# Both heads of a pair in the two halves of the rows: 64x64 tiles of TensorE in a chunked attention, without block-diagonal copies

## The chip, the cores and the metric

One core of a Trainium2 chip runs the whole program. The metric is device microseconds of one execution; the time before is 1209.59 us, the median of 3 runs (1208.75 to 1212.22). Engines: PE is TensorE, DVE VectorE, ACT ScalarE, POOL GpSimd; SP only issues DMAs here.

## The reference

A recurrent attention feeds a mixture of experts, and that feeds a two-layer network. With 4 batches, 8 heads, 768 steps and head size 40:

```
for t in range(S):
    y[:, :, t] = einsum('bhd,bhde->bhe', r_t, state)
    Sa = einsum('bhde,bhe->bhd', state, a_t)
    state = state*w_t[:, :, None, :] - outer(Sa, b_t) + outer(v_t, k_t)
```

`y` as 3072 tokens of 320 is routed to one of 8 experts (320 to 1024 to 320, ReLU, scaled by the gate's probability), and the result goes through 320 to 2048 to 320 with a leaky ReLU. All is float32.

## The kernel before

**The attention** (class `Attn`, lines 536 to 890) cuts the 768 steps into 12 chunks of 64. The 32 heads are 16 pairs; `E`=40 is the head size, and a pair lies in `PW`=104 columns, head 0 in 0 to 39 and head 1 in 64 to 103. Chunks are worked two at a time (`kk`, 6 rounds in `run`, line 860). In a round:

- `a_load` and `kb_load` (643 to 661) load a, k and b with time on the rows and multiply them by running products of w (`pro`, `prod`). `K` has k in rows 0 to 63 and b in rows 64 to 127.
- `s1a` (662), for each of four groups of 4 pairs, transposes a on PE and copies the result out twice: into `abd`, a block-diagonal form in which each head's 64 columns have zeros at the other head's rows (two copies of 40x512), and into rows 64 to 103 of `XL` (four copies of 40x256).
- `s1` (678), for a chunk and a group, transposes K, copies it to `kbT`, and multiplies it by `abd` with all 128 rows: rows 0 to 63 of the result are masked into `XL` on DVE, rows 64 to 127 are copied and sent through memory (`LTd`) to the solver.
- `solver2` (704) turns all 32 heads of both chunks by substitution: 62 DVE instructions one after the other. `g_out` and `g_load` (709, 743) take the result through memory into `Gr`, for each pair a block-diagonal 128x128 matrix, and `wg` (767) fills its off-diagonal 32x32 blocks with matmuls on 32x32 tiles.
- `chain` (792), for a chunk and a group z of 4 pairs, carries the state. It has six steps on PE with evictions between them: transposes of v and r; transposes of the state `D0`; v and state times r (`VD`, `rb`, 4 matmuls, 104 columns of weights, 128 moving); `XL` times `R1` (8 matmuls of 128 rows and 64 columns); `Gr` times `X` (4 matmuls, 128x128); `K` times `R1` (8 matmuls of 128 rows and 64 or 40 columns). `R1` holds one head per column block, v's part in rows 0 to 63 and the state's part below, so the state and v are copied into it, and r is copied into `rb` in block-diagonal form. DVE masks, adds the state and writes `Y`; the decay goes to POOL or DVE.

A float32 matmul is two MATMUL passes in the trace, each with its own weight load.

**The experts** (class `Moe`, from 893) load weights in pieces into two buffers `raw`, split them in two parts (copies and subtractions on ACT, DVE, POOL) into three slots `w0`, `w1`, `w2`, and run PE. The same columns hold the attention's buffers before: `raw` and `abd` share columns of the region `pe`, and the slots hold `K`, `XL`, `Gr` and the solver's tiles.

**The order** is a list planner's (`Sched`, from line 100): every operation has a cost (`cost`, 183), a priority from a backward pass, and is put where it can start first. `copy` may go to ACT or DVE, `copy3` to ACT, DVE or POOL, `pv` to POOL or DVE; `tensor_tensor` on `nc.vector` stays on DVE. The matmuls of one step are one block and go out together. PSUM is 8 banks of 512 columns. Everything is emitted from lines 527 (blocks) and 529 (all else), so the trace's lines tell only these two apart and shapes tell the rest.

## Time and profile before

| what | value |
|---|---|
| median of 3 runs | 1209.59 us |
| the profiled execution | 1210.86 us, of which its span is 1209.0 us |
| busy, share of the span | PE 83%, PE's weight loads 74%, DVE 68%, ACT 53%, POOL 31% |
| instructions | 23474, of which MATMUL passes 8757 |
| mean granted clock of PE | 0.932 |
| DMA | 113.71 MB in 255413 packets |

How to read it: busy times are unions on one engine. The attention fills the first 560 us or so, the experts and the network the rest. A group of instructions is a line of code, an engine, an operation, names (w, f, plain are the slots and the plain region; bank is PSUM) and a shape; behind the bar stand its busy time in us, the mean of one in ns and the idle time before.

### The profile page before, as it was taken

Reading aid. Unit: us, or ns where it says so; the run is one execution under the profiler, and the core shown is the slowest. Engines: PE = TensorE matmul, PEld = TensorE weight load, DVE = VectorE, ACT = ScalarE, POOL = GpSimd, SP = SyncE. Lnnn points to the kernel's source line nnn. Section 1 sums busy time; section 2 is a strip of 40 time slices with the busy share of each in tenths; the row PEclk is TensorE's granted clock in tenths of the full one; section 3 lists DMA queues with packets and bytes.
Section 4 is the critical chain, followed back from the end, with each engine's and each line's share of the span. In section 5 each row is a group of like instructions: output and inputs, shape, how many; then the busy total and the mean of one; then the engine's idle time right before and its main releaser. Section 6 shows DMA issues by size and latency. Waiting matters only on the chain.

```text
span 1209.0 us, 23474 instructions
## 1 busy us (share of the span) xinstructions
PE 1009.3 (83%) x8757; PEld 897.0 (74%) x8757; DVE 826.9 (68%) x1681; ACT 641.9 (53%) x1473; POOL 376.8 (31%) x587
## 2 busy tenths in 40 slices
PE   2553787787877879789799999877999999999994
PEld 1352676676766767777699998867899999999994
DVE  5788687976879867757655559979655555555561
ACT  7885987797885968665544444434121212121230
POOL 9684266463553121222111112334001010110231
PEclk9875998989898989899799999987999999999998
DMA  9454365747638464933844444342100000000000
GB/s 163 110 152 112 77 103 109 141 93 145 107 80 174 76 141 114 253 89 113 217 130 133 126 113 120 109 147 82 66 1 23 11 22 18 17 6 17 12 7 31
DMA packets 255413, 113.71 MB, mean 94 GB/s; under 512 B 206784, under 2 KB 242416, under 8 KB 255097
## 3 DMA queue, kind: packets, MB, share of 16 engines
q1 hardware_dynamic: 251449, 100.25, 36.4%
q0 software_dynamic: 3840, 11.85, 2.9%
q8 instruction: 71, 1.16, 0.4%
q14 instruction: 53, 0.43, 0.1%
HBM read 81.08 MB, written 35.98 MB: 97 GB/s over the span
## 4 chain that ended last, share of the span: by engine, by line
PE 51%; ACT 15%; DVE 14%; DMA 8%; issue 5%; POOL 4%; SPq 2%; POOLq 0%; DVEq 0%; ACTq 0%
PE bank L529 41%; PE bank L527 11%; ACT w L529 8%; DVE plain L529 7%; DVE w L529 5%; ACT plain L529 5%; ACT f L529 2%; SPq L529 2%; DMA plain<-in_moe_w_in_dram 2%; DVE f L529 2%; POOL w L529 2%; DMA out_dram<-plain 1%; POOL f L529 1%; POOL plain L529 1%; DMA plain<-xs 1%
## 5 line engine op out<-in xcount | busy, mean ns | idle before, releaser
L529 PE MATMUL bank<-f,w 128*128 128x512 f32 (+2 forms) x1472 | 330.9, 365 | 6.7 <-ACT f L529 3.5
L529 PE MATMUL bank<-w,f 128*128 128x320 f32 (+1 forms) x1824 | 313.8, 314 | 10.7 <-ACT f L529 9.1
L529 PEld LDWEIGHTS bank<-w,f 128*128 128x128 f32 (+1 forms) x1824 | 284.7, 189 | 24.0 <-ACT f L529 10.8
L529 PEld LDWEIGHTS bank<-f,w 128*128 128x128 f32 x1472 | 254.3, 192 | 38.5 <-ACT f L529 4.3
L527 PE MATMUL bank<-plain,w 128*64 128x104 f32 (+3 forms) x1664 | 164.1, 280 | 51.6 <-ACT w L529 21.5
L527 PEld LDWEIGHTS bank<-plain,w 128*128 128x128 f32 (+2 forms) x1664 | 143.7, 170 | 70.9 <-ACT w L529 27.7
L529 ACT CAST f<-plain 128x512 fp32r<-128x512 f32 (+1 forms) x96 | 56.2, 586 | 240.1 <-PE bank L529 215.7
L529 DVE TENSOR_TENSOR w<-w 128x135 f32<-128x135 f32 (+20 forms) x401 | 154.3, 388 | 16.7 <-DMA w<-LTd 6.5
L529 DVE TENSOR_SCALAR plain<-bank,plain 128x512 f32<-128x512 f32 (+2 forms) x114 | 76.5, 672 | 123.4 <-PE bank L529 121.9
L529 ACT COPY w<-bank 40x256 f32<-40x256 f32 (+5 forms) x323 | 138.4, 436 | 23.2 <-PE bank L527 17.8
L529 DVE TENSOR_TENSOR plain<-bank,w 64x256 f32<-64x256 f32 (+2 forms) x192 | 87.6, 462 | 58.4 <-ACT f L529 19.0
L529 ACT COPY plain<-bank 104x256 f32<-104x256 f32 (+6 forms) x222 | 92.1, 432 | 25.9 <-PE bank L527 13.2
L529 POOL TENSOR_TENSOR w<-w 128x120 f32<-128x120 f32 (+4 forms) x133 | 93.5, 719 | 31.1 <-ACT w L529 19.0
L527 PE MATMUL bank<-ident,w 128*104 128x128 f32 x384 | 61.4, 297 | 39.5 <-POOL w L529 26.8
L529 ACT CAST w<-plain 128x640 fp32r<-128x640 f32 (+4 forms) x105 | 60.4, 591 | 63.4 <-DVE plain L529 29.6
L529 POOL DMA_INDIRECT ys<-plain x32 | 43.6, 1361 | 150.3 <-ACT plain L529 80.1
L527 PEld LDWEIGHTS bank<-ident,w 128*104 128x104 f32 x384 | 46.7, 141 | 46.2 <-POOL w L529 31.7
L529 DVE TENSOR_TENSOR w<-plain,w 128x512 fp32r<-128x512 f32 (+3 forms) x97 | 63.2, 655 | 24.4 <-ACT w L529 21.1
L529 POOL DMA_INDIRECT out_dram<-plain x24 | 25.9, 1079 | 151.3 <-ACT plain L529 110.7
L529 DVE SCALAR_TENSOR_TENSOR plain<-bank,plain 128x512 f32<-128x512 f32 (+1 forms) x112 | 68.5, 613 | 4.4
L529 ACT ACTIVATE f<-bank 128x480 fp32r<-128x480 f32 (+1 forms) x72 | 37.8, 530 | 63.3 <-PE bank L529 62.5
L529 DVE SCALAR_TENSOR_TENSOR f<-bank,f 128x480 fp32r<-128x480 f32 (+1 forms) x72 | 42.9, 601 | 36.3 <-ACT f L529 36.2
(110 smaller groups left out, 1334.9 us busy)
## 6 DMA issues: line engine op xcount, KB each, us to landing
plain<-in_moe_w_dram SPq DMA_DIRECT2D x32, 320.0 KB, 3.5
plain<-in_moe_w_dram SPq DMA_DIRECT2D x64, 128.0 KB, 2.7
LTd<-w SPq DMA_DIRECT2D x40, 128.0 KB, 2.3
plain<-in_moe_w_out_dram SPq DMA_DIRECT2D x8, 640.0 KB
xs<-w SPq DMA_DIRECT2D x8, 608.8 KB
plain<-xs SPq DMA_DIRECT2D x7, 603.8 KB, 5.4
plain<-in_moe_w_in_dram SPq DMA_DIRECT2D x8, 512.0 KB, 5.1
ys<-in_moe_w_dram SPq DMA_DIRECT2D x1, 3864.0 KB, 15.2
```

The source lines that it names most:

```text
L527: for _,m,a,k in a[0]: getattr(nc.tensor,m)(*[f(x) for x in a],**{q:f(x) for q,x in k.items()})
L529: getattr(getattr(nc,e),m)(*[f(x) for x in a],**{q:f(x) for q,x in k.items()})
```

## The change

The two heads of a pair get the two halves of the rows everywhere, and every product of the attention is made on 64x64 tiles: a row half holds one head's weights, a column half takes one result. What was one matmul over 128 rows with a zero block, or over two stacked operands, becomes several over 64 or 40 rows; sums over two operands are two accumulating matmuls.

```diff
 def s1a:
-        abd=s.abd0[b] if kk==0 else s.abd()
-        s.S.copy(abd[0:40,:,:,0,:],pv[0:40]); s.S.copy(abd[64:104,:,:,1,:],pv[64:104])
         for q in range(2):
-            s.S.copy(XLb[64:104,:,0,:],pv[0:40,:,q,:]); s.S.copy(XLb[64:104,:,1,:],pv[64:104,:,q,:])
+            s.S.copy(s.XL[(2*kk+q)%s.NK][0:PW,b*4:b*4+4,0,:],p2[0:PW,:,64*q:64*q+64])
 def s1:
-        p3=s.ps([128,4,128])
+        p3=[s.ps([128,4,64]) for _ in range(2)]
             for p in range(4):
-                nc.tensor.matmul(p3[:,p,:],kbT[:,p,:],abd[:,p,q].rearrange("p h n -> p (h n)"),start=True,stop=True)
-        nc.vector.tensor_tensor(XL[0:64,b*8:b*8+8,:],p3v[0:64],s.maskV[0:64].unsqueeze(1).to_broadcast([64,8,64]),op=ALU.mult)
+                for i in range(2):
+                    for h in range(2):
+                        o=64*(h^i); nc.tensor.matmul(p3[i][o:o+64,p,:],kbT[64*h:64*h+E,p,o:o+64],XL[64*h:64*h+E,p,0,:],start=True,stop=True)
+        nc.vector.tensor_tensor(XL[:,:,1,:],p3[0],s.maskV[:,0].unsqueeze(1).to_broadcast([128,4,64]),op=ALU.mult)
-        nc.sync.dma_start(out=s.LTd[c][:,b*8:b*8+8,:],in_=L.rearrange("p (c t) -> p c t",t=64))
+        if not up: L=s.LT(); s.S.copy(L,p3[1])
+        for h in range(2):
+            if up: s.S.copy(s.slots(s.Ld[64*(c%2):64*(c%2)+64],k)[:,2*b:2*b+2],two(p3[1][o:o+64]))
+            else: nc.sync.dma_start(out=s.slots(s.LTd[c],k)[:,2*b:2*b+2],in_=two(L[o:o+64]))
 def g_load:
-                nc.sync.dma_start(out=s.Gr[c%2][o:o+32,:,o:o+32],in_=s.GPd[c][blk*32+h:blk*32+32:2].rearrange("q s t -> s q t"))
+                for u in range(2): nc.sync.dma_start(out=s.Gr[c%2][o:o+32,u::2,32*blk:32*blk+32],in_=s.GPd[c][blk*32+2*k+u:blk*32+32:4].rearrange("n s t -> s n t"))
 def vr_load:
-                nc.sync.dma_start(out=x[:,:,64*q:64*q+E],in_=y[2*q:2*q+2,:,sl,:].rearrange("b h t e -> t (b h) e"))
+                for h in range(2): nc.sync.dma_start(out=V[64*h:64*h+64,i,:,64*q:64*q+E],in_=y[2*q:2*q+2,h::2,sl,:].rearrange("b h t e -> t (b h) e"))
 def chain (the new body, in order):
+            for i in range(2):
+                for a in range(2): nc.tensor.transpose(p[0:PW,i,a,:],V[:,i,2*z+a,:],s.ident)
+        VD=s.VD(); cp(VD[0:PW],p[0:PW])
+        s.S.copy3(two(R1[:,0],64),two(V[:,0,2*z:2*z+2]))
+            for a in range(2): nc.tensor.transpose(p[0:PW,a,:],R1[0:PW,1,a,64:64+PW],s.ident[0:PW,0:PW])
+        ST=s.ST(); cp(ST[0:PW,:,0:PW],p[0:PW])
+        p=[s.ps([128,2,2,64]) for q in range(2)]
+            for a in range(2):
+                for i in range(2):
+                    for h,q,_ in hq:
+                        o=slice(64*h,64*h+64); nc.tensor.matmul(H(p[q],h)[:,i,a,:],H(ST,q,E)[:,a,o] if i else H(VD,q,E)[:,0,a,o],H(VD,q,E)[:,1,a,o],start=True,stop=True)
+        for q in range(2): nc.vector.tensor_tensor(R1[:,:,:,168*q:168*q+64],p[q],s.maskV.unsqueeze(2).to_broadcast([128,2,2,64]),op=ALU.mult)
+        p=[s.ps([128,2,PW]) for q in range(2)]
+            for a in range(2):
+                for i in range(2):
+                    for h,q,k in hq:
+                        n=E if i else 64; nc.tensor.matmul(H(p[q],k)[:,a,:],H(XL,h,n)[:,g(a,q),1-i,:],H(R1,h,n)[:,i,a,128*q:128*q+PW],start=i==0,stop=i==1)
+        for q in range(2): cp(X[q],p[q])
+        p=[s.ps([128,2,PW]) for q in range(2)]
+            for a in range(2):
+                for h,q,k in hq: nc.tensor.matmul(H(p[q],1-h)[:,a,:],H(Gr,k)[:,g(a,q),:],H(X[q],k)[:,a,:],start=True,stop=True)
+        for q in range(2): nc.vector.tensor_tensor(X[q],p[q],s.maskU[:,q].unsqueeze(1).to_broadcast([128,2,PW]),op=ALU.mult)
+        p=[s.ps([128,4,PW]) for q in range(2)]
+            for a in range(2):
+                for q in range(2):
+                    for i in range(2):
+                        for h in range(2):
+                            n=64 if h==0 else E; nc.tensor.matmul(H(p[i],h,n)[:,2*a+q,:],H(K,h^i)[:,g(a,q),64*h:64*h+n],H(X[q],1-h)[:,a,:] if i else H(R1,h)[:,0,a,128*q:128*q+PW],start=True,stop=True)
+        nc.vector.tensor_tensor(x,two(A,0,PW,PW),x,op=ALU.add)
+        if c<NC-1:
+            nc.vector.tensor_tensor(x,two(B,64,40),x,op=ALU.add)
+            s.S.pv('tensor_tensor',x,x,P.unsqueeze(3).to_broadcast([PW,2,2,E]),op=ALU.mult)
+        nc.vector.tensor_tensor(Y[0:PW],two(B,0,144,64),two(T,0,168,64),op=ALU.add)
 buffers and planner:
-        s.abd=Rot([t('pe',1024,4,2,2,64)]); s.P2=t('pe',1280,32,E)
+        vd=lambda w: t(w,512,2,2,128); s.VD=Rot([vd('pe'),vd('pe'),vd('w2'),vd('w2')]); s.P2=t('pe',1280,32,E)
-            if op.cls==(32,32): t=40
+            if op.cls==(32,32): t=20
+                r=(region(s.rv(q[2][1]))[0] if o.cls[0]<128 else 0,region(s.rv(q[2][0]))[0] if o.cls[1]<128 else 0) if o.cls[0]>32 else 0
```

Here `H(x,h,n)` is the n rows of x from 64h on, `g(a,q)` the pair, and `hq` lists the four tiles as (h, q, h xor q). `prod` covers both heads with one instruction where it had two. Steps that write both row halves take two PSUM banks at once, and the planner's rule for free banks is extended to that; its test for overlapping tiles also becomes finer. The list of buffers to be zeroed at the start loses `abd`, `rb`, `D0` and parts of others and gains the state's part of `R1`. `b` lies in `K` with its heads' halves exchanged.

## Rows read from the trace of the kernel before

**Rows 1.** Busy time by stage: us, PE, PEld, DVE, ACT, POOL, granted clock, DMA share, GB/s

```profile
0.00:160.00 160.00, 80.10 (x767) 62.70 (x771) 117.09 (x220) 126.42 (x257) 96.29 (x217) 0.83 0.60 124
160.00:560.00 400.00, 328.09 (x4478) 281.61 (x4469) 304.50 (x757) 306.96 (x820) 158.76 (x253) 0.92 0.58 121
560.00:600.00 40.00, 28.95 (x185) 26.09 (x183) 28.30 (x93) 19.81 (x49) 8.52 (x11) 0.83 0.81 216
600.00:1209.00 609.00, 572.14 (x3349) 526.56 (x3348) 377.01 (x614) 188.72 (x349) 113.23 (x108) 0.97 0.20 60
```

**Rows 2.** The chain of waits in 160 to 560 us, shares by engine and line

```profile
by line: PE bank L527 27.1%; ACT w L529 13.0%; DVE w L529 12.3%; ACT plain L529 10.4%; DVE plain L529 8.3%; issue 8.2%; SPq L529 4.0%; PE bank L529 3.2%; ACT f L529 2.7%; DMA w<-GPd 1.7%; DVE f L529 1.5%; DMA plain<-in_b_dram 1.4%; DMA w<-i
```

**Rows 3.** Busy time in two neighbouring stretches of 40 us, columns as in group 1

```profile
320.00:360.00 40.00, 33.24 (x328) 28.00 (x329) 28.74 (x67) 36.53 (x98) 26.38 (x39) 0.96 0.40 83
360.00:400.00 40.00, 30.74 (x533) 25.22 (x529) 37.26 (x97) 26.23 (x69) 11.91 (x17) 0.91 0.73 142
```

**Rows 4.** Groups of instructions by shape in 160 to 560 us: ACT

```profile
L529 ACT COPY w<-bank 40x256 f32<-40x256 f32 x128 | 46.9, 366 | 1.6
...
L529 ACT ACTIVATE plain<-bank 64x160 f32<-64x160 f32 x88 | 26.1, 298 | 28.5 <-DVE plain L529 26.5 <-issue 0.5
L529 ACT COPY plain<-f 40x160 f32<-40x160 f32 x77 | 24.4, 322 | 12.9 <-POOL f L529 11.4
...
L529 ACT COPY plain<-bank 128x416 f32<-128x416 f32 x43 | 21.7, 508 | 5.2 <-PE bank L527 2.5 <-issue 1.0 <-ACT w L529 0.8
...
L529 ACT COPY plain<-bank 40x512 f32<-40x512 f32 x30 | 17.4, 580 | 1.2 <-PE bank L527 0.6
L529 ACT COPY w<-bank 104x512 f32<-104x512 f32 x29 | 16.4, 587 | 3.2 <-PE bank L527 2.7
...
L529 ACT COPY plain<-bank 104x256 f32<-104x256 f32 x42 | 15.7, 373 | 1.6 <-PE bank L527 1.0
...
L529 ACT COPY plain<-bank 128x160 f32<-128x160 f32 x41 | 11.9, 294 | 2.2 <-PE bank L527 1.7
```

**Rows 5.** Groups of instructions by shape in 160 to 560 us: DVE

```profile
L529 DVE TENSOR_TENSOR plain<-bank,w 64x256 f32<-64x256 f32 x88 | 37.1, 423 | 22.4 <-PE bank L527 12.0 <-ACT plain L529 8.0 <-issue 0.5
...
L529 DVE TENSOR_TENSOR plain<-bank,w 104x512 f32<-104x512 f32 x44 | 30.1, 685 | 17.6 <-ACT f L529 14.7 <-PE bank L527 2.4
...
L529 DVE TENSOR_TENSOR f<-bank,f 104x256 f32<-104x256 f32 x44 | 18.1, 414 | 0.7 <-PE bank L527 0.6
...
L529 DVE TENSOR_TENSOR w<-bank,w 64x512 f32<-64x512 f32 x23 | 15.6, 679 | 7.1 <-PE bank L527 4.0 <-ACT w L529 2.9
...
L529 DVE TENSOR_TENSOR w<-bank,f 104x160 f32<-104x160 f32 x40 | 12.7, 317 | 0.6 <-PE bank L527 0.3
```

**Rows 6.** Timeline of PE: start, duration, rows*columns of weights, moving form, passes

```profile
393.38 0.75 PE L527 MATMUL bank<-w,w 32*32 32x32 f32 x64
...
456.51 2.06 PE L527 MATMUL bank<-plain,w 128*128 128x104 f32 x16
...
459.12 1.91 PE L527 MATMUL bank<-w,plain 128*104 128x128 f32 x16
460.97 1.64 PE L527 MATMUL bank<-plain 128*64 128x104 f32 x32
```

**Rows 7.** Busy time in two neighbouring short stretches, columns as in group 1

```profile
484.10:487.50 3.40, 1.75 (x16) 1.59 (x15) 2.34 (x4) 2.31 (x6) 1.47 (x1) 0.99 0.69 113
487.50:490.90 3.40, 3.40 (x18) 3.40 (x17) 3.21 (x10) 1.28 (x5) 0.12 (x1) 0.50 0.85 205
```

**Rows 8.** Timeline: the solver on DVE, SP's issues for one chunk, PE around the attention's end

```profile
79.53 23.37 DVE L529 TENSOR_TENSOR w<-w 128x31 f32<-128x31 f32 x62
...
442.73 2.76 SPq L529 DMA_DIRECT2D w<-GPd  x5
...
503.78 4.63 PE L529 MATMUL bank<-f,w 128*128 128x256 f32 x24 [3.52 <-ACT f L529]
...
584.51 1.54 PE L529 MATMUL bank<-ident,plain 128*128 128x128 f32 x6 [4.11 <-DMA plain<-xs]
```

More of the change, by code (lines that the diff above doesn't have):

```diff
@@ L77, in region @@
         elif a%per: per=0; break
-    m=(per,c0%per,L) if per and c0%per+L<=per else None
-    return (p0,p1,c0,c1,m,per is None and dense)
+    m=(per,c0%per,L) if per and L<=per else None
+    runs=None; L=es; n=1; R=[c0]
+    for a,k in d:
+        if n==1 and a==L: L*=k
+        elif n*k<=16: n*=k; R=[x+a*i for i in range(k) for x in R]
+        else: break
+    else: runs=(tuple(R),L)
+    return (p0,p1,c0,c1,m,per is None and dense,runs)
 def overlap(x,y):
@@ L85, in overlap @@
         if t%s==0:
-            b%=s
-            if b+m<=s and (a+l<=b or b+m<=a): return False
+            if (b-a)%s>=l and (a-b)%s>=m: return False
+    if x[6] and y[6]: return any(a<b+y[6][1] and b<a+x[6][1] for a in x[6][0] for b in y[6][0])
     return True
@@ L366, in psum_ok1 @@
         def psum_ok1(o):
-            for vt in o.vts:
-                if vt.bank is None: break
-            else: return scat.get(o.sc,0.0) if o.sc else 0.0
+            new=[v for v in o.vts if v.bank is None]
+            if not new: return scat.get(o.sc,0.0) if o.sc else 0.0
+            vt=new[0]; need=len(new)
             used=[h for h in held if h is not None]
@@ L374, in psum_ok1 @@
             elif vt.cls!='u':
-              for q in vt.ops:
-                for p in q.preds:
-                    if p.eng is None and vt not in p.vts: return None
-            fr=[bankfree[b] for b in range(len(held)) if held[b] is None]
-            if len(fr)<s.RES and fr:
+              for w in new:
+                for q in w.ops:
+                  for p in q.preds:
+                    if p.eng is None and not any(x in p.vts for x in new): return None
+            fr=sorted(bankfree[b] for b in range(len(held)) if held[b] is None)
+            if len(fr)<need: return None
+            if len(fr)<s.RES+need-1:
                 while bypri and bypri[-1].eng is not None: bypri.pop()
                 if o.pri<bypri[-1].pri-s.RESP: return None
-            return min(fr) if fr else None
+            return fr[need-1]
         bypri=sorted(ops,key=lambda o:o.pri); tick={}; warm={0:False}
@@ L547, in __init__ @@
         s.AT=t('w0',16*PW,16,PW)
-        lt=[t('w0',512) for _ in range(2)]; s.LT=Rot([lt[0][64:128],lt[1][64:128],lt[0][0:64],lt[1][0:64]])
+        s.LT=Rot([t('w0',256,4,64) for _ in range(4)])
         s.W0=t('w0',1320,33,E); s.Wn0=s.W0[:,1:33]; s.rpn=t('w0',1280,32,E); s.RP=t('w0',1280,32,E)
@@ L641, in put, with two @@
         for h in range(2):
-            s.nc.sync.dma_start(out=dst[:,:,64*h:64*h+E],in_=src[:,h::2].rearrange("b h t e -> t (b h) e"))
+            s.nc.sync.dma_start(out=dst[h][:,:,64*h:64*h+E],in_=src[:,h::2].rearrange("b h t e -> t (b h) e"))
+    @staticmethod
+    def two(x,o=0,d=64,n=E):
+        f=lambda x: bass.AP(x.tensor,x.offset+o,[list(y) for y in x.ap[:-1]]+[[d,2],[1,n]])
+        return x.via(f) if isinstance(x,VP) else f(x)
     def kb_load(s,c):
         s.S.cur=f'kb{c}'
-        nc=s.nc; sl=slice(c*64,c*64+64); K=s.KB[c%s.NK]
-        s.put(K[0:64],s.k[:,:,sl,:]); s.put(K[64:128],s.b[:,:,sl,:])
+        nc=s.nc; sl=slice(c*64,c*64+64); K=s.KB[c%s.NK]; l=[K[0:64],K[64:128]]
+        s.put(l,s.k[:,:,sl,:]); s.put(l[::-1],s.b[:,:,sl,:])
         RP=s.RPs() if c<4 else s.RP; x=64*(c%2); s.turned(RP[0:64],s.PR[c//2][1][x:x+64])
@@ L651, in prod @@
         for q in range(4):
-            for h in range(2):
-                x=K[:,4*q:4*q+4,64*h:64*h+E]
-                s.S.pv('tensor_tensor',x,x,P4[:,4*q:4*q+4,h],op=ALU.mult)
+            x=s.two(K[:,4*q:4*q+4]); s.S.pv('tensor_tensor',x,x,P4[:,4*q:4*q+4],op=ALU.mult)
     def a_load(s,kk):
@@ L781, in wg @@
         for j in range(4):
-            h=64*(j%2)
-            s.S.copy(Gr[h:h+32,j//2::2,h+32:h+64],ph[32*j:32*j+32])
+            h=64*(j//2)
+            s.S.copy(Gr[h:h+32,j%2::2,32:64],ph[32*j:32*j+32])
     def vr_load(s,c):
@@ L796, in chain @@
-        AQ=[(a,q,2*a+q,8*q+2*z+a) for a in range(2) for q in range(2)]
-        p=s.ps([128,4,128])
+        nc=s.nc; V=s.VR; cp=s.S.copy; R1=s.R1[z]; two=s.two; X=s.X[z]; K=s.KB[c%s.NK]; XL=s.XL[c%s.NK]; Gr=s.Gr[c%2]
+        Y=s.Y[z].rearrange("p (a q c n) -> p a q c n" if c<NC-2 else "p (a c q n) -> p a q c n",a=2,c=2,q=2)[:,:,:,c%2]
+        hq=[(h,q,h^q) for h in range(2) for q in range(2)]; H=lambda x,h,n=64: x[64*h:64*h+n]; g=lambda a,q: 8*q+2*z+a
+        p=s.ps([128,2,2,128])
         with s.S.block():
-            for j in range(4): nc.tensor.transpose(p[0:PW,j,:],V[:,o+j,:],s.ident)
```

119 lines of the change are left out of this document (36 added, 83 removed).

## The prediction, made blind

> **What bounds the kernel now.** I read the table by stage first [rows 1]. From 600 us on PE is busy 572 of 609 us: that part is the experts' and the change does not touch its instructions, so whatever the attention gains or loses moves it as a whole. From 160 to 560 us, the attention's steady part, nothing is full: PE 328, DVE 304.5 and ACT 307 of 400 us. The chain of waits there [rows 2] says the same: PE about 30%, ACT about 26%, DVE about 22%, SP's issues 4%. Two neighbouring stretches show why [rows 3]: in one ACT is busy 36.5 of 40 us and DVE 28.7, in the next DVE 37.3 and ACT 26.2, PE 33.2 and 30.7. The solver's 62 instructions in a row [rows 8] fill DVE, then the chains' copies fill ACT. So the two take turns, with PE close behind, and a cut in ACT's work pays in ACT's turns until PE or DVE is full there.
>
> **ACT's copies.** Per chain and group the kernel now copies 4 pieces of 40x256 (r into its block-diagonal form, the y part), one of 104x256, four of v and state (40x160 and the like, 322 ns), two negations of 64x160, one of 128x160 and one of 128x416: 4x366 + 373 + 4x322 + 2x298 + 294 + 508 = 4523 ns [rows 4]. After, there are VD (104x512, 587), v (322), the transposed state (104x208) and two of X (128x208). For 208 columns there is no row; between 294 (160 columns) and 373 (256) I take 334. Sum 587 + 322 + 3x334 = 1911, so 2.61 us less. `s1a` loses two copies of 40x512 and four of 40x256, 2x580 + 4x366 = 2624, and gets two of 104x256, 746: 1.88 us less. `s1`'s copy of 64x512 (nearest row 104x512, 587) becomes one of 128x256 (nearest 104x256, 373): 0.21 less; in chunks 0 and 1 it becomes two of 64x256 instead, no gain. The stage holds 44 chains (the 104x512 masks [rows 5]), 15 `s1a` (30 copies of 40x512 [rows 4]) and 31 `s1` (23 masks of 64x512 in the row [rows 5], eight under another name). ACT falls from 307 to 307 - 115 - 28 - 7 = 157 us.
>
> **DVE.** What was a negation or a copy on ACT is now part of a DVE instruction. Per chain before: 685 + 2x423 + 317 + 414 = 2262 ns [rows 5]. After: two masks of 128x256 (423 each), two of 128x208 (between 317 and 414: 366 each), the sum into state and y (104x416, between 414 and 685, by its columns 583), the state's second sum (317) and y (414): 2892, so 0.63 us more. `s1`'s mask goes from 679 to 423, 0.26 less. In the stage DVE goes from 304.5 to 304.5 + 44x0.63 - 31x0.26 = 324 us. It becomes the fullest engine; copies that the planner now puts on DVE can go to ACT, which I do not count. `prod` halves its instructions on POOL, busy 159 of 400 us [rows 1]: no gain, no cost, and if POOL's slack were gone the same products would still be fewer.
>
> **PE.** A pass costs 1.91/16 = 119 ns with 128 moving columns, 2.06/16 = 129 on the full array with 104, and 1.64/32 = 51 where two column halves alternate [rows 6]. A chain's products are 8x119 + 8x129 + 32x51 = 3.62 us now, an `s1`'s 8x119 = 0.95. After, a chain has 56 small matmuls, 112 passes (24 matmuls, 48 passes before), an `s1` 32 passes for 8. No row has a 64x64 pass. From below it is bounded by the 32x32 blocks, 0.75/64 = 11.7 ns a pass; from above by the column pair's 51, if the row halves bring nothing. I take 26, half of 51: a pass moves the same columns as the pair's and twice as many tiles run, and the 32x32 blocks show tiles of different row groups overlapping. Then a chain is 2.91 and an `s1` 0.83 us, and PE goes from 328 to 328 - 44x0.70 - 31x0.12 = 293 us; with 11.7 it is 208, with 51 it is 441. Transposes stay. The 32x32 blocks also answer another question: their four row groups write one bank at the same time, in different rows of it, and reach those 11.7 ns.
>
> The Trainium skill, "TensorEngine Tiling (Array Packing)", Restrictions and Gotchas, says that different row tiles cannot access the same PSUM bank simultaneously. In `s1` and in the `XL`, `Gr` and `K` steps of the new chain each bank is written by both row halves; by that rule two tiles at most would run at a time and PE would come to 441 us and the kernel to 1285, by the trace's 32x32 blocks to 293 and 1172.
>
> **SP.** `s1` issues two DMAs for one, `g_load` 14 for 10 per chunk, `vr_load` 8 for 4: 24 more in a round of two chunks. One costs 2.76/5 = 0.55 us on SP [rows 8], so 13 us a round of some 80. Bytes are the same. SP's queue is in order, so behind `Gr`'s loads, which wait for the solver's result to land, stand the next chunk's k, b and w and the weights' pieces; POOL's products wait for those, then PE's transposes. SP is 4% of the chain [rows 2]; I price this at nothing in the forecast, covered by PE's and DVE's work on the other groups, and at four issues on the path of every chunk, 2.2 us x 10 chunks = 22 us, if that cover is gone.
>
> **PSUM.** Four of six steps and `s1` now ask for two free banks at once. Where fewer are free, a block waits and its engine takes another group. No row prices it; it stands in how full I let DVE become.
>
> **Sum.** DVE's 324 us set the steady stage. DVE fills 76% of it now and 93% in its own turn [rows 1, 3]. Without ACT's turns it should come near the upper; but the solver still runs alone and the other steps still wait for PE. At 87.5% the stage is 370 us, 30 less; at 93% 348, 52 less; at 81% nothing is gained. PE at 293 of 370 is as full as now. In the first 160 us ACT is the fullest, 126 us [rows 1]. It loses 8x1.88 for two rounds of `s1a` and 4x2.61 for chunk 0, 25 us. The solver [rows 8] and the loads are not shortened, so I take half, 12 (0 to 25). The shorter list of zero fills I count at nothing, under the first loads. At the end the new `VD` lies in columns of `raw` until the last chunk has read it, so part of expert 0's weights is split later, and the PE work that now runs at 504 us [rows 8] falls into the stage to 600. PE idles 11 of 40 us there, and expert 1 starts only when the routed rows have landed, at 584.5 [rows 8]. I take 3 (0 to 10). Against the profiled execution's own 1210.9 us, 1.3 above the median and inside the runs' spread: 1210.9 - 12 - 30 + 3 = 1172.
>
> **Rivals.** First, **two tiles at a time** (slower). If the two row halves of a block take turns, a pass costs 51 ns and PE's 441 us become the bound; filled to 93% the stage is 474 us, 74 longer, and with 3 at the end and nothing won at the start the kernel takes about 1285. The place is the four steps of the chain and `s1`. It decides from 39 ns a pass on: 189 us of products become 5920 passes, and at 39 PE needs 372 of 400. Against it stand the 32x32 blocks [rows 6], for it that no 64-row tile is in the trace. I give it 0.16. Its rule is the one of the Trainium skill, "TensorEngine Tiling (Array Packing)", told above.
>
> Second, **a colder PE**. In one short stretch PE was busy 1.75 of 3.4 us, and in the next the granted clock was 0.50, the 1.2 GHz level; 18 passes then took all 3.4 us, 189 ns each, against 119 at 2.4 GHz [rows 7, 6]. The stage's mean of 0.92 is 16% of the time at the low level. Small tiles do each step in less time, so PE pauses more. At a mean of 0.72 PE's 293 us become 374, at 93% a stage of 402: with 6 won at the start and 3 lost at the end about 1210. 0.09.
>
> Third, **SP on the path**: 1172 + 22, about 1195. 0.08.
>
> Fourth, **DVE packs as in its turns**: 348 us for the stage, 20 at the start, 1210.9 - 52 - 20 + 3, about 1142. For it: ACT at 157 us is never in the way. 0.17.
>
> **How the numbers follow.** The forecast keeps 0.50, from 1150 to 1190 by the ends of its terms. The range leaves out the first rival and the ends of the fourth: 1130 to 1216. A measurement can tell about 0.3%, 3.6 us. Faster: 0.50 + 0.17 + 0.08 and 0.02 of the colder PE, 0.77. Same: 0.04 of it. Slower: 0.03 of it and 0.16, 0.19.
>
> **What would show it.** Right: in the steady stage ACT's busy time near 160 us, DVE's near 325 and its share above 85%; 64x64 passes at 20 to 32 ns in the timeline; the solver's 62 instructions as long as before. Wrong: passes of 40 ns or more and PE the fullest; a granted clock below 0.8; SP's share of the chain well over 4%; DVE's share still under 80%, which would say that latencies or banks and not DVE set the pace; or a stage after 600 us that is longer than 609.

## The result, and the profile after

The changed kernel takes **1167.49 us** (median of 4 runs, 1163.75 to 1168.5), against 1209.17 for the kernel before in the same runs: a ratio of 0.9654, with a 95% interval of 0.9614 to 0.9695. The profiled execution took 1168.5 us, its span 1166.7; before it was 1210.86 and 1209.0. The forecast was 1172.

To say where the 42.3 us of span went, a mark is needed that both kernels have. DVE's sum into `Y`, 104x256, stands 48 times in each, once for a chunk and a group. The timeline of the changed kernel, its first and its last, and PE's first transposes of routed rows after them (start, duration, engine, what):

```profile
144.15 0.41 DVE L539 TENSOR_TENSOR f<-bank,plain 104x256 f32<-104x256 f32 x1
...
508.69 0.41 DVE L539 TENSOR_TENSOR f<-bank,plain 104x256 f32<-104x256 f32 x1
...
535.73 0.69 PE L539 MATMUL bank<-ident,plain 128*128 128x128 f32 x2 [2.83 <-DMA plain<-xs]
```

The kernel before, its first and last of the same instruction:

```profile
147.11 0.41 DVE L529 TENSOR_TENSOR f<-bank,f 104x256 f32<-104x256 f32 x1
...
558.56 0.42 DVE L529 TENSOR_TENSOR f<-bank,f 104x256 f32<-104x256 f32 x1 [0.60 <-PE bank L527]
```

PE's row of before is in [rows 8], 584.51. So the start went from 147.1 to 144.2 us (-3.0), the **steady part from first to last sum from 411.5 to 364.5 us (-46.9)**, the wait for the routed rows from 26.0 to 27.0 (+1.1), and the rest to the end of the span from 624.5 to 631.0 (+6.5). The busy times in these stretches, before (columns as in [rows 1]):

```profile
147.11:558.56 411.45, 335.83 (x4664) 288.34 (x4661) 314.85 (x786) 317.33 (x852) 160.71 (x257) 0.93 0.58 121
...
558.56:584.51 25.95, 15.94 (x100) 13.59 (x99) 21.58 (x78) 13.89 (x34) 8.10 (x9) 0.84 0.73 205
584.51:1209.00 624.49, 586.60 (x3442) 540.10 (x3442) 385.18 (x630) 196.08 (x366) 114.53 (x111) 0.97 0.22 64
```

and after, with the first 160 us of [rows 1] on top:

```profile
0.00:160.00 160.00, 110.72 (x1889) 78.81 (x1894) 128.65 (x229) 84.83 (x200) 107.97 (x228) 0.73 0.72 140
...
144.15:508.69 364.54, 294.18 (x7902) 233.59 (x7903) 299.39 (x808) 167.75 (x428) 139.94 (x211) 0.87 0.61 128
...
508.69:535.73 27.04, 18.95 (x133) 16.23 (x133) 23.25 (x94) 16.12 (x42) 9.36 (x12) 0.94 0.71 206
535.73:1166.70 630.97, 587.39 (x3442) 541.73 (x3442) 383.06 (x619) 194.21 (x367) 122.43 (x121) 0.97 0.22 64
```

In the steady part ACT fell from 317 to 168 us, PE from 336 to 294, DVE from 315 to 299. These are unions: the records of neighbouring instructions on one engine overlap. Added up one by one, the instructions come to 337 and 184 us on ACT and to 345 and 353 on DVE, so DVE's work did not shrink; 54 us of it overlap after, 30 before. As shares of the part: ACT 77% to 46%, PE 82% to 81%, DVE 77% to 82%. PE's mean granted clock fell from 0.93 to 0.87, and in the first 160 us from 0.83 to 0.73. After 536 us PE does the same 587 us of work as before in a stretch that is 6.5 us longer, so it idles more there.

The chain of waits of the changed kernel from 145 to 520 us, its steady part and 11 us more, which answers to [rows 2]:

```profile
by line: PE bank L537 36.1%; DVE w L539 11.6%; issue 10.4%; SPq L539 8.8%; DVE plain L539 8.3%; DMA w<-GTd 4.3%; PE bank L539 4.1%; DMA xs<-plain 2.2%; ACT w L539 1.8%; DMA w<-in_v_dram 1.4%; DMA plain<-in_b_dram 1.3%; DVE f L539 1.2%; DMA 
```

ACT's 26% are down to 3% (1.8% on `w`, the rest in smaller entries behind the end of the line), PE has risen from 30 to 40%, and SP's issues have doubled from 4.0 to 8.8%. Groups by shape in the steady part, DVE and then ACT, as in [rows 4, 5]:

```profile
L539 DVE TENSOR_TENSOR plain<-bank,w 128x256 f32<-128x256 f32 x88 | 35.1, 415 | 8.2 <-PE bank L537 7.3 <-issue 0.6
L539 DVE TENSOR_TENSOR plain<-bank,w 128x208 f32<-128x208 f32 x77 | 26.7, 364 | 4.5 <-PE bank L537 4.0 <-ACT plain L539 0.4
L539 DVE TENSOR_TENSOR plain<-bank,plain 104x416 f32<-104x416 f32 x44 | 25.7, 584 | 4.8 <-PE bank L537 4.4
```

```profile
L539 ACT COPY plain<-bank 128x208 f32<-128x208 f32 x77 | 22.3, 334 | 36.4 <-PE bank L537 34.5 <-DVE plain L539 1.3 <-issue 0.4
...
L539 ACT COPY f<-bank 104x208 f32<-104x208 f32 x41 | 13.5, 336 | 12.3 <-PE bank L537 9.5 <-DVE plain L539 2.0 <-PE bank L539 0.6
```

And passes of TensorE, as in [rows 6]; the first two stood at a granted clock of 1.00, the third in 2 us with a mean of 0.60:

```profile
236.12 0.69 PE L537 MATMUL bank<-f,w 40*64 40x64 f32 x32
...
434.26 0.90 PE L537 MATMUL bank<-plain,w 64*64 64x104 f32 x32
...
476.29 1.86 PE L537 MATMUL bank<-plain,w 64*64 64x104 f32 x32
```

A block of 32 passes of 40x64 takes 0.69 us, 21.6 ns a pass; one of `XL` or `K` (64x104) takes 0.90, 28 ns, or 1.86 (58 ns) where the clock is down. At the upper clock neither has the 51 ns of the first rival.

### The profile page after: what moved, and what is told of

It reads as the page before. It is cut to its first block, busy times and chain, and to the rows that moved or that the text cites. A ratio compares the mean times of both kernels' runs of the same rounds, so it can differ in the third digit from the quotient of the medians.

```text
span 1166.7 us, 31904 instructions
## 1 busy us (share of the span) xinstructions
PE 995.6 (85%) x13038; PEld 857.3 (73%) x13051; DVE 818.5 (70%) x1712; ACT 455.0 (39%) x1015; POOL 365.8 (31%) x550
## 4 chain that ended last, share of the span: by engine, by line
PE 57%; DMA 13%; DVE 12%; issue 6%; SPq 6%; ACT 3%; POOL 3%; POOLq 0%; DVEq 0%; ACTq 0%
PE bank L539 42%; PE bank L537 14%; DVE w L539 7%; SPq L539 6%; DVE plain L539 5%; DMA ys<-plain 3%; ACT w L539 2%; DMA w<-GTd 1%; POOL w L539 1%; DMA out_dram<-plain 1%; DMA xs<-plain 1%; DVE f L539 1%; ACT f L539 1%; DMA plain<-in_moe_w_in_dram 1%; DMA w<-in_r_dram 1%
## 5 line engine op out<-in xcount | busy, mean ns | idle before, releaser
L539 DVE TENSOR_TENSOR w<-w 128x135 f32<-128x135 f32 (+20 forms) x401 | 174.6, 438 | 9.3 <-DMA w<-LTd 2.8
L539 ACT COPY w<-bank 104x512 f32<-104x512 f32 (+8 forms) x243 | 104.5, 445 | 84.2 <-PE bank L537 61.4
L539 ACT CAST w<-plain 128x512 fp32r<-128x512 f32 (+4 forms) x107 | 61.3, 578 | 97.2 <-PE bank L539 42.8
L537 PE MATMUL bank<-ident,w 128*104 128x128 f32 x384 | 68.3, 322 | 33.9 <-POOL w L539 11.5
L539 DVE TENSOR_TENSOR plain<-bank,w 128x208 f32<-128x208 f32 (+2 forms) x228 | 80.8, 376 | 20.6 <-PE bank L537 16.2
L537 PE MATMUL bank<-plain,w 64*64 64x104 f32 (+2 forms) x2416 | 86.7, 278 | 5.7 <-issue 2.8
L539 POOL TENSOR_TENSOR plain<-plain,w 104x160 f32<-104x160 f32 (+4 forms) x63 | 49.4, 789 | 130.9 <-DVE plain L539 104.5
L539 DVE TENSOR_TENSOR w<-plain,w 64x256 fp32r<-64x256 f32 (+3 forms) x96 | 59.9, 627 | 40.6 <-ACT w L539 33.4
L537 PEld LDWEIGHTS bank<-plain,w 64*64 64x64 f32 (+2 forms) x2416 | 71.8, 147 | 19.4 <-issue 8.7
L539 ACT COPY plain<-bank 128x208 f32<-128x208 f32 (+4 forms) x140 | 49.1, 392 | 60.4 <-PE bank L537 48.0
L537 PE MATMUL bank<-w,w 32*32 32x32 f32 (+3 forms) x2608 | 53.2, 225 | 18.3 <-ACT w L539 4.9
```

Of the source, the lines that this page charges most:

```text
L537: for _,m,a,k in a[0]: getattr(nc.tensor,m)(*[f(x) for x in a],**{q:f(x) for q,x in k.items()})
L539: getattr(getattr(nc,e),m)(*[f(x) for x in a],**{q:f(x) for q,x in k.items()})
```

## The experiments

All steady parts below are measured between the same two sums into `Y`, in one profile each; the times are medians, and the ratios are against the kernel before on the same chip. In the kernels that leave work out (less ACT, less PE, both, the shorter products of the changed kernel, no products of `K`) the result is not the reference's, and a constant (`thr`) is set besides, so that the program does not go on to its slow second way of computing all of it. The time from PE's first routed rows to the end, with the same 3442 passes or nearly so, lay between 615 and 631 us in the kernels here, so up to some 15 us of a difference in the steady part can be lost or added behind it.

**The control.** Every kernel that changes an operation is put in order anew by the planner, so first: how much does a new order alone move?

```diff
-Sched.BIAS=300.0
+Sched.BIAS=305.0
```

> A control: the changed kernel with one constant of the planner moved from 300 to 305, the same instructions in another order. It says how far a new order alone moves the time, which bounds what may be read from the other runs that plan anew. Expected under every theory: within 8 us of 1167.5, with ACT's and DVE's busy time in 130 to 515 us within 5 us of 179 and 319. If it is off by 20 us or more, the gain of the change is itself partly a matter of the order.

1176.71 us, ratio 0.974 (0.9696 to 0.9784). The steady part:

```profile
147.75:520.90 373.15, 305.82 (x7963) 243.42 (x7955) 293.19 (x818) 171.56 (x434) 138.00 (x203) 0.82 0.62 129
```

It is 373.2 us long, 8.6 more than in the changed kernel, and the whole time is 9.2 longer, just outside of the 8 expected and a fifth of the gain. So an order alone can move the time by some 9 us, and of these two draws the changed kernel had the better one. How far other orders would move it, one control does not tell. What follows is held against both.

**ACT's relief and PE's relief, each alone and together, on the kernel before.**

```diff
 less ACT:
-        cp(rb[0:40,:,0,:],p[0:40,:,64:128]); cp(rb[64:104,:,1,:],p[64:104,:,64:128])
+        if c==0 and z<2: cp(rb[0:40,:,0,:],p[0:40,:,64:128]); cp(rb[64:104,:,1,:],p[64:104,:,64:128])
-        for h in range(2): cp(Y[64*h:64*h+E],...)
+        for h in range(2 if c<2 else 0): cp(Y[64*h:64*h+E],...)
-        s.S.copy(abd[0:40,:,:,0,:],pv[0:40]); s.S.copy(abd[64:104,:,:,1,:],pv[64:104])
+        if kk==0: s.S.copy(abd[0:40,:,:,0,:],pv[0:40]); s.S.copy(abd[64:104,:,:,1,:],pv[64:104])
 less PE (hi takes the upper 16 bits of each number as bfloat16):
-                    nc.tensor.matmul(p[h*64:h*64+n,i,:],K[:,g,64*h:64*h+n],R1[:,4*a+2*h+q,:],start=True,stop=True)
+                    nc.tensor.matmul(p[h*64:h*64+n,i,:],hi(K[:,g,64*h:64*h+n]),hi(R1[:,4*a+2*h+q,:]),start=True,stop=True)
```

> The kernel before with less work on ACT and nothing else: the block-diagonal copies of r are made for the first two groups only, those of a in the first round only, and the copies of y's part in the first two chunks only, so that y and the solver's input are not the reference's from there on. In the steady stage that is 44 x 1.46 + 15 x 1.16 = 82 us less of the 306 on ACT; PE's and DVE's work stays. Theory A (the prediction's: ACT's turns are what the change removed): 25 to 35 us shorter than before, 1175 to 1185. Theory P (PE's shorter products gave the gain): within 8 us of before. Theory C (PE, ACT and DVE are each about 79% full, and a relief of one alone leaves the other two): 5 to 15 us shorter.

> The kernel before with shorter products and nothing else: in the chain's last product step (K) only the upper halves of the float32 numbers are multiplied, in one pass for two, so its low halves are left out. By the 51 ns of a pass of that step this is 44 x 16 x 0.051 = 36 us less on PE in the steady stage, about what the change was reckoned to take off PE; ACT and DVE keep their work. Theory P: 25 to 45 us shorter than before. Theory A: within 8 us of before. Theory C: 5 to 15 us shorter.

> Both reliefs at once on the kernel before (ACT's 82 us and PE's 36 us; what they leave out is the same as in the two kernels alone). Theory A: as the one with less work on ACT. Theory P: as the one with shorter products. Theory C: clearly more than either, and more than their sum of 10 to 30 us: 30 to 45 us shorter than before, so near the changed kernel.

Less ACT: 1193.57 us, ratio 0.9893 (0.9842 to 0.9944). Less PE: 1209.08, ratio 1.0012 (0.9977 to 1.0047). Both: 1194.09, ratio 0.9888 (0.9833 to 0.9943). Their steady parts, less ACT:

```profile
152.76:536.62 383.86, 315.11 (x4540) 276.93 (x4538) 299.61 (x721) 249.61 (x666) 161.06 (x261) 0.91 0.64 130
```

less PE:

```profile
152.85:562.43 409.58, 316.81 (x4174) 271.59 (x4173) 314.42 (x789) 306.54 (x815) 160.26 (x263) 0.88 0.58 121
```

and both:

```profile
143.34:537.07 393.73, 315.13 (x4144) 269.63 (x4132) 305.65 (x750) 247.10 (x662) 153.38 (x249) 0.87 0.62 124
```

ACT has 68 us less (82 were reckoned), and DVE 15 less, which had made some of these copies. The steady part of 411.5 us shrinks to 383.9, by 27.6, and no shorter product is in it. Not all of it need be ACT's: PE is busy 21 us less there too, as some 120 of its passes lie outside of the two marks now. In the whole kernel only some 15 us of it arrive: the first sum comes 5.7 us later than before, and PE's routed rows 8.3 us later after the last. So by the whole time Theory A's 25 to 35 us are missed, and the 14.6 lie at the upper end of what Theory C gave to one relief. PE's relief alone brings nothing (1.9 us of the steady part), as Theory A had it, and on top of ACT's nothing either, so Theory P falls as the whole cause and Theory C's larger sum isn't there. Neither A nor C holds as it was stated. One thing was wrong in the expectation: `K` has 16 passes a chain and loses 8, not 16. PE's busy time fell by 19 us, half of the 36 meant, at a clock of 0.88 for 0.93, so a relief of full size was not tried. The timeline shows `K` of two chains, 8 passes each; of the first, one stands 0.8 us ahead of the 7 shown:

```profile
393.60 0.35 PE L527 MATMUL bank<-plain,w 128*40 128x104 bf16 x7 [0.63 <-ACT plain L529]
...
396.13 0.38 PE L527 MATMUL bank<-plain,w 128*64 128x104 bf16 x8
```

**ACT's load put back in the changed kernel.**

```diff
-        VD=s.VD(); cp(VD[0:PW],p[0:PW])
+        for _ in range(3): s.nc.scalar.copy(VD[0:PW],p[0:PW])
-        ST=s.ST(); cp(ST[0:PW,:,0:PW],p[0:PW])
+        for _ in range(2): s.nc.scalar.copy(ST[0:PW,:,0:PW],p[0:PW])
-        for q in range(2): cp(X[q],p[q])
+        for q in (0,1,0,1,0,1): s.nc.scalar.copy(X[q],p[q])
 (s1a's two copies also twice)
```

> Undoes the relief of ACT alone: the changed kernel, with its copies of VD made three times, of ST twice, of X three times (2.84 us more for each chain) and those of s1a twice, all kept on ACT, so that ACT's work in the steady stage is again near the 307 us it had before; values are the same, TensorE's small products and DVE's work stay. Theory 1 (the gain came from ACT's turns): most of it is lost, 1195 to 1215, and ACT is back in the chain of waits of the steady stage with over 12%. Rival (the gain came from PE's shorter products): at most 10 us over the control. Rival (ACT's time is covered, only the latency of single copies counted): 5 to 15 us.

1180.4 us, ratio 0.9766 (0.9727 to 0.9804). The steady part, and its chain of waits:

```profile
146.65:534.97 388.32, 320.81 (x8119) 251.40 (x8118) 296.30 (x830) 265.90 (x771) 137.93 (x208) 0.85 0.62 128
```

```profile
by line: PE bank L537 44.4%; DVE w L539 9.8%; ACT w L539 8.0%; issue 6.5%; ACT plain L539 5.6%; DVE plain L539 4.8%; PE bank L539 3.8%; DMA w<-in_b_dram 2.6%; SPq L539 2.3%; DMA LTd<-w 2.0%; ACT f L539 1.8%; DMA w<-in_v_dram 1.6%; DMA w<-LT
```

The steady part is 388.3 us, 23.8 longer than in the changed kernel and 15.2 longer than in the control. Added up one by one ACT's instructions are back at 335 us (337 before), but copies made again right behind each other overlap, so ACT is busy for 266 us, 68%, not the 77% of before. It has 15% of the chain of waits (8.0 + 5.6 + 1.8), as Theory 1 asked. By the whole time the kernel can't be told from the control (3.7 us longer, the intervals overlap): it misses the 1195 of Theory 1 and lies in the 10 us of the rival that gives the gain to PE. So ACT's load counts in the steady part, though the relief was not undone in full, and the time behind it makes up for most: the stretch from the routed rows to the end is 13 us shorter than in the changed kernel.

**PE's products made longer in the changed kernel.** The order of the matmuls inside a block is all that is changed; the rest of the plan is the same, so no new draw is in it: in the traces of these kernels and of the changed one, DVE's 1712, ACT's 1015 and POOL's 550 instructions stand in the same order. In all five steps:

```diff
 s1, and in the same manner the chain's first step, XL, Gr and K:
-            for p in range(4):
-                for i in range(2):
-                    for h in range(2):
+            for h in range(2):
+                for p in range(4):
+                    for i in range(2):
                         o=64*(h^i); nc.tensor.matmul(p3[i][o:o+64,p,:],kbT[64*h:64*h+E,p,o:o+64],XL[64*h:64*h+E,p,0,:],start=True,stop=True)
```

> The same instructions, the same plan, but inside each block the matmuls of one row half stand before those of the other (s1, and the four product steps of the chain), so that only the two column halves can run side by side. If the four tiles of the changed kernel run at once because neighbours lie in different row halves, a pass rises from 22 to 28 ns to 45 to 51, a block of 32 passes from 0.7 to 0.9 us to 1.4 to 1.6, PE becomes the fullest engine in the steady stage (400 us or more of work) and the kernel takes 1240 to 1285. Rival (the order in a block does not matter, the row halves overlap anyhow across the pairs): within 5 us of the changed kernel.

1202.54 us, ratio 0.9951 (0.9922 to 0.998).

```profile
155.38:560.19 404.81, 383.12 (x7930) 321.53 (x7929) 295.83 (x808) 169.71 (x431) 141.65 (x211) 0.74 0.55 115
```

PE is busy 383 of 404.8 us, 95%: it is the bound, as expected, and by the medians 35 of the 42 us are lost (the profiled execution, 1212.6, was among the longest of ten). But the kernel is not at 1240. Then in `XL` and `K` alone:

> The changed kernel, the same plan, with the row halves in turn in two of its steps only (XL and K, 64 of a chain's 112 passes). By the 33 ns that a 64x64 pass took with row halves in turn at the upper clock, against 22 to 28 ns, that is 5 to 11 ns for each of 2816 passes, 14 to 31 us more on PE in the steady stage, so PE's work is about what it was before the change. If PE's shorter products are the part of the gain that ACT's relief does not explain: 12 to 25 us longer than the changed kernel, 1180 to 1192. If they are not: at most 6 longer.

1182.52 us, ratio 0.9806 (0.976 to 0.9853).

```profile
144.94:522.20 377.26, 338.75 (x7912) 281.39 (x7906) 299.33 (x808) 168.98 (x432) 141.04 (x212) 0.81 0.59 124
```

This is 15.0 us longer than the changed kernel, and the intervals are apart. The steady part is 377.3 us, 12.7 longer at the same plan, with PE at 339 us (336 before the change), 45 more than in the changed kernel where 14 to 31 were reckoned, at a clock of 0.81; the profiled execution, 1175.8, was the shortest of four. A block of `XL` or `K` in this kernel:

```profile
444.33 1.32 PE L537 MATMUL bank<-plain,w 64*64 64x104 f32 x32
```

41 ns a pass. It and the 0.90 us block of the changed kernel were both at the upper clock, the first of these rows the changed kernel's, the second this one's (columns as in [rows 1], the clock before the DMA share):

```profile
434.00:438.90 4.90, 4.90 (x171) 3.93 (x162) 4.70 (x14) 2.62 (x7) 0.00 (x0) 1.00 0.63 148
```

```profile
444.20:445.70 1.50, 1.50 (x59) 1.37 (x52) 1.47 (x6) 0.38 (x2) 0.00 (x0) 1.00 0.51 118
```

So 28 ns with neighbours in different row halves against 41 in turn: the order is worth a third of a pass, not half. (These figures are a block's time by its passes, the last one's end included. From start to start, over all such runs of 14 passes or more, the median is 22.7 ns in the changed kernel and 34.5 in this one, a third as well.) The 32 weight loads of the two blocks, the changed kernel's first, shrink alike:

```profile
434.20 0.75 PEld L537 LDWEIGHTS bank<-plain,w 64*64 64x64 f32 x32
...
444.27 1.17 PEld L537 LDWEIGHTS bank<-plain,w 64*64 64x64 f32 x32
```

Whether the products themselves or their weight loads gain by the order is not separated. With PE's load of before, PE takes the chain of waits over:

```profile
by line: PE bank L537 63.2%; DVE w L539 7.6%; PE bank L539 5.7%; issue 5.3%; DVE plain L539 4.5%; ACT w L539 2.9%; SPq L539 2.5%; DMA plain<-in_b_dram 1.4%; DMA f<-in_b_dram 1.3%; DMA w<-in_b_dram 1.1%; DMA w<-GTd 1.0%; POOL f L539 0.8%; DM
```

**Both loads put back:** the copies on ACT made again as above, and the row halves in turn in `XL` and `K`, together.

> The two together: XL and K with the row halves in turn, and ACT's copies repeated as in act_full. PE's and ACT's loads are then both near those before the change, DVE's is above it by the 20 us of the change. If these two loads are the whole gain: 1195 to 1212, about the kernel before. If they are not (the shape of the chain, fewer and larger evictions, counts for itself): 1180 to 1192.

```profile
148.30:555.90 407.60, 361.92 (x8119) 294.38 (x8118) 297.50 (x830) 266.60 (x772) 136.80 (x208) 0.81 0.59 122
```

The median is 1199.66 us, but three of its four executions took 1199.3 to 1202.1, the profiled one among them, and one took 1181.4; no interval comes of that. The first three would be the first answer of the expectation, the fourth is the second, so both stay possible, and the row is not held against the others.

**PE's products shorter still.** `XL` and `K` in one pass for two in the changed kernel, with `hi` around both operands as above.

> The changed kernel with the two steps XL and K in one pass for two (upper halves only, the low halves left out): 32 passes less a chain, by 22 to 28 ns each 31 to 39 us less on PE in the steady stage; DVE's and ACT's work as in the changed kernel. If DVE alone sets the pace of the changed kernel: 0 to 8 us shorter than it. If PE sets it with DVE, or alone: 12 to 35 us shorter. With the spread that a new order brings (9 us in the control), only more than 12 counts.

1157.59 us, ratio 0.9624 (0.9551 to 0.9697).

```profile
143.70:503.43 359.73, 277.63 (x6566) 205.13 (x6567) 294.05 (x817) 167.26 (x428) 143.35 (x215) 0.78 0.62 131
```

The steady part is 359.7 us, 4.8 shorter. PE's busy time fell by 17 us only, where 31 to 39 were reckoned; its mean clock is 0.78 instead of 0.87. The interval covers the changed kernel's 0.9654; no gain can be told.

**DVE's load, more and less.** The masks of the chain's first step made twice, and in another kernel cut to the columns that need them, with ACT doing the others:

```diff
 twice:
-        for q in range(2): nc.vector.tensor_tensor(R1[:,:,:,168*q:168*q+64],p[q],...)
+        for q in (0,1,0,1): nc.vector.tensor_tensor(R1[:,:,:,168*q:168*q+64],p[q],...)
 less:
+            nc.vector.tensor_tensor(R1[:,0,:,168*q:168*q+64],p[q][:,0],...)
+            nc.scalar.copy(R1[:,1,:,168*q:168*q+64],p[q][:,1])
...
+            nc.vector.tensor_tensor(X[q][:,:,m],p[q][:,:,m],...)
+            nc.scalar.activation(X[q][:,:,u],p[q][:,:,u],AF.Copy,scale=-1.0)
```

> Doubles a part of DVE's load: the two masks of 128x256 of the chain's first step are made twice, 0.83 us more for each of 48 chains, some 40 us in all, 36 of them in the steady stage. Theory 1 (DVE now sets the pace at 83 to 87% busy): 25 to 45 us longer, 1192 to 1212, DVE's share of the stage about what it is now. Rival (PE and latencies set the pace and DVE has room): up to 12 us longer, DVE's share of the stage up to 92%.

1196.57 us, ratio 0.9907 (0.9875 to 0.994): 29 us longer than the changed kernel, 20 longer than the control, for some 40 us of work. That is in the range of Theory 1.

```profile
144.55:542.85 398.30, 325.90 (x8009) 252.09 (x8009) 326.18 (x903) 178.78 (x440) 146.83 (x214) 0.81 0.58 121
```

> The changed kernel with DVE's masks cut to the columns that need one: of the first step's result the state's half (where the mask is all ones) is copied by ACT, and of the second mask's 104 columns the 40 that are only negated go to ACT. The result is the same. By 1.2 ns a column DVE loses 2 x 150 + 2 x 94 = 490 ns a chain, 21 us in the steady stage, and ACT, 47% busy, gets four instructions of some 280 ns, 49 us. If DVE sets the pace there (doubling its first masks cost 20 to 29 us for 40): 8 to 15 us faster than the changed kernel, 1152 to 1160. If DVE's work is not what counts: within the 9 us that a new order brings, 1160 to 1176.

1178.2 us, ratio 0.9746 (0.972 to 0.9773): 11 us **longer** than the changed kernel, 1.5 longer than the control.

```profile
142.95:536.95 394.00, 320.32 (x8186) 255.03 (x8176) 281.95 (x850) 208.91 (x623) 138.13 (x218) 0.82 0.62 129
```

Both kernels have longer steady parts than the control: 398.3 us with DVE at 326 (82%), and 394.0 with DVE at 282 (72%) and ACT at 209 (53%). The first alone would say that DVE sets the pace, though the doubled masks also lengthen every chain's own path. The second does not bear it out: 17 us less on DVE, and no gain. It is no clean counter-test either, because it puts four more instructions a chain on ACT, and two steps of every chain then wait for ACT as well as for DVE; what that costs was not tried. So whether DVE's work or the length of a chain's path counts here stays open.

**POOL beside the solver.** In the changed kernel's profile the first solver's 62 instructions took 11.3 and 16.0 us, against 23.4 in one piece before [rows 8], with two transposes between them:

```profile
67.41 11.31 DVE L539 TENSOR_TENSOR w<-w 128x31 f32<-128x31 f32 x29
78.64 2.68 DVE L539 STREAM_TRANSPOSE w<-w 64x1280 f32<-64x1280 f32 x1
81.35 2.69 DVE L539 STREAM_TRANSPOSE f<-w 64x1280 f32<-64x1280 f32 x1
84.07 15.97 DVE L539 TENSOR_TENSOR w<-w 128x255 f32<-128x255 f32 x33
```

and POOL's products with the running products of w stood beside the second half (POOL's timeline):

```profile
82.69 2.68 POOL L539 TENSOR_TENSOR plain<-plain,w 128x320 f32<-128x320 f32 x3 [4.75 <-ACT w L539]
...
88.34 1.04 POOL L539 TENSOR_TENSOR plain<-plain,w 128x320 f32<-128x320 f32 x1
89.34 1.04 POOL L539 TENSOR_TENSOR plain<-plain,f 128x320 f32<-128x320 f32 x1
```

```diff
-        s.S.copy(RP[64:128],RP[0:64]); s.prod(K,RP)
+        s.S.copy(RP[64:128],RP[0:64])
+        if c<2: s.prod(K,RP)
```

> The changed kernel without POOL's products of k and b with the running products of w from chunk 2 on (so the attention's result is not the reference's): this takes away what POOL does beside the solvers. If POOL's work beside them is what lengthened the solver's instructions, the first solver's two halves fall from 32 us to 23 to 26 us, the 128x252 mean from 723 ns to 450 to 580, and the kernel is 8 to 20 us faster than the changed one. If the instructions are long for another reason (their operands' places), the solver stays at 30 us or more and the kernel within 5 us, or as much faster as POOL's own turns in the chain give.

1168.8 us, ratio 0.9661 (0.9636 to 0.9685): no faster. The steady part, and the first solver:

```profile
144.60:521.38 376.78, 311.05 (x8070) 249.80 (x8068) 285.48 (x823) 168.29 (x435) 112.00 (x178) 0.84 0.63 130
```

```profile
64.41 14.05 DVE L539 TENSOR_TENSOR w<-w 128x31 f32<-128x31 f32 x36
...
80.96 11.46 DVE L539 TENSOR_TENSOR w<-w 128x247 f32<-128x247 f32 x26
```

The 128x252 mean fell from 723 to 414 ns, below what the first theory said, but the kernel did not move. The first solver's two halves, with what stands between them, went from 32.6 to 28.0 us, not to the 23 to 26 of that theory. This solver ends 7.6 us sooner: 3.0 because it starts sooner, 2.8 because one transpose and not two stands in the middle, and 1.8 because its instructions are shorter (14.1 + 11.5 for 11.3 + 16.0). The first sum into `Y` stands at 144.6 us all the same, where the changed kernel has it. This kernel is in a new order, too, and beside the solver's second half POOL still makes four 128x320 products (of other tiles), so POOL's part is not shown apart from the order's.

## Why the prediction was right, and where it was not

**The sum** was 1210.9 - 12 - 30 + 3 = 1172, and the sign, the size and the range held. Its terms erred against each other: -3.0 at the start, -46.9 in the steady part, +7.6 behind it. That the sum came within 5 us is in part luck; each of the three was off by 5 to 17.

**ACT** was right in size: -150 us forecast, 317.3 - 167.8 = 149.6 measured; the sizes read between rows were right too (128x208: 334 ns). That its turns bound is borne out by the kernel with less ACT, -27.6 us of the steady part, and by its share of the chain of waits, 26% to 3%. But that kernel took only 68 of the 150 us off ACT, and 15 off DVE with them, 14.6 us of it reach the whole time, and putting load back in the changed kernel lengthened the steady part by 15 to 24 and the whole time by 13, of which a new order can be 9. So ACT's relief is a cause, and its size is not settled.

**PE.** The price of a pass, 26 ns, was good (21.6 and 28). But the forecast gave PE's cut no share of the gain, since PE "at 293 of 370 is as full as now". It was as full (294 of 364.5, 81%), and for that very reason its cut was needed: with PE's load of before, at the same plan, 12.7 us of the steady part and 15.0 of the whole time are lost, and PE has 63% of the chain of waits. The 27.6 us of the one run and the 12.7 of the other come to 40 of the steady part's 47, but they were measured in different kernels and orders, and the run with both loads put back, which was to close this sum, stayed undecided; so the split is not shown. A cut of full size in PE's work alone, on the kernel before, was not tried. In the sum for the first rival a pass of 39 ns gives 370 us, not 372.

**The step that failed** is "DVE's 324 us set the steady stage". The single durations were as estimated (364 and 584 ns for 366 and 583), but DVE's busy time fell by 15 us where 20 more were forecast, and its share is 82%, not 87.5%. That lies between the 85% that the prediction named as a sign of being right and the 80% that it named as one of being wrong. Of the tests, more work on DVE lengthened the stage, less work didn't shorten it, and neither is clean; what lengthened it at the same plan is PE's passes. The miss of 35 us in DVE's busy time can be read from the groups by shape. Some 13 us were copies that the change does without and that DVE had made before, which the forecast put on ACT alone or did not count; the largest group of them (steady part of the kernel before):

```profile
L529 DVE COPY f<-bank 40x256 f32<-40x256 f32 x20 | 8.5, 427 | 0.5
```

With them the forecast of +20 becomes +7, and added up one by one DVE's instructions did rise by 8, from 345 to 353 us. The other 24 us are overlap: the sum added single durations, while neighbouring records overlap by 30 us before and by 54 after. (The stretches are not quite the same, 400 us forecast, first to last sum measured.)

**The start**, -12 forecast, brought 3.0. Its solver started 12.1 us sooner (67.4 for 79.5) and ended 2.9 sooner (100.0 for 102.9), though the prediction's sign of being right was that its 62 instructions take as long as before: two transposes in their midst took 5.4 us, and the instructions themselves 3.9 more (27.3 for 23.4), some of them beside POOL's products. In the kernel without these products the solver ended 7.6 us sooner and the first sum came no sooner, so what holds the first chain stays open. **The tail and the rest**, +3 with a bound of 10, came to +7.6.

**The rivals.** *Two tiles at a time* did not happen, and its price was too high. "It decides from 39 ns" was about right: with the halves in turn in all steps, at a clock of 0.74, PE fills 95% of the steady part. But the 51 ns of the column pair, read from tiles of 128 rows, was not what two tiles of 64 rows cost, and the time came to 1202.5 instead of 1285. The rule of the Trainium skill, "TensorEngine Tiling (Array Packing)", Restrictions and Gotchas, that different row tiles cannot access one PSUM bank simultaneously, did not bind here for tiles that write different rows of the bank: in `K` both row halves write each bank, and a pass takes 28 ns where it takes 41 with the halves in turn; the 32x32 blocks [rows 6] speak against it too. How much of the 13 ns is the weight loads' is open, as said. (The trace of before does have passes with 64 rows of weights, 44 of 64*32 in the steady part, but none on 64x64 tiles.) *A colder PE* came in part: the clock of the steady part fell to 0.87, not to 0.72. *SP* has 8.8% of the chain, twice its share of before; by the prediction's own words that speaks for the rival, and no run put it alone to the test. In the control, with the same DMAs in another order, SP has 4.5% of the steady part's chain and the time is 9 us longer, so the share says little of the price. *DVE packed to 93%* was not seen.

## What to carry to other kernels

A relief of 150 us on the engine that took turns with two others, with 42 on PE, was worth 47 of the steady part and 42 of the whole; the first is not the second, so look at both. Single durations add up to more than an engine is busy, because neighbouring records overlap. Before experiments are read on a planner's kernel, a control with a new order and the same instructions shows what an order alone can do, here 9 us for one draw; an edit that keeps the plan needs none. Such an edit is the order of small matmuls inside a block: in this kernel it was worth 35 us to have neighbours in different row halves.
